# A pre-norm block with hedgehog linear attention and a gated FFN: four re-orderings in the opening, the key/value loop and the FFN

## The chip, the cores and the metric

The kernel runs on one core of a Trainium2 chip. The metric is the device time of one execution in microseconds (us). The times before are three runs of the same kernel; one further execution was taken by the hardware profiler and left the profile that is read here. Engines are named as the profile names them: PE is TensorE (PEld its weight loads), DVE is VectorE, ACT is ScalarE, POOL is GpSimd, SP is SyncE, which issues the DMAs.

## The reference

The input `x` has 2048 rows of 640 numbers, all tensors are bfloat16. There are 32 heads of 20 numbers, and the FFN is 1536 wide.

```python
ln = layernorm(x)                                   # over 640, no scale or shift
q, k, v = split_heads(ln @ wqkv)                    # 32 heads of 20
pq, pk = q @ w_phi[h], k @ w_phi[h]                 # per head, 20 x 20
phi_q = concat([softmax(pq), softmax(-pq)], -1)     # 40 numbers for each head
phi_k = concat([softmax(pk), softmax(-pk)], -1)
kv  = einsum("bhsf,bhsd->bhfd", phi_k, v)           # summed over all 2048 rows
z   = einsum("bhsf->bhf", phi_k)
num = einsum("bhqf,bhfd->bhqd", phi_q, kv)
den = einsum("bhqf,bhf->bhq", phi_q, z)[..., None] + 1e-6
h   = x + (num / den) @ wo
out = h + (gelu(layernorm(h) @ w_gate) * (layernorm(h) @ w_up)) @ w_down
```

The attention is not causal: every row's `phi_q` needs `kv` summed over all rows. So all 16 tiles must have passed the key/value stage before the first row's attention can be finished.

## The kernel before, in words

The 2048 rows are 16 tiles of 128 rows, four tiles to a block. A tile `t` passes these steps in the first half of the kernel:

- `ln_st` (lines L109 to L127) takes the statistics of one or two tiles. For a pair it is four `bn_stats` and two `bn_aggr` on DVE, then on POOL `ve` (variance plus eps, L121), `rstd` (L122) and one `mr` for each tile (L127).
- `ln_ap` applies the normalisation, in one instruction on ACT (L133) or DVE (L138). Its result is transposed into `LN1T`, either by a DMA that SP issues (L149) or, for the first tiles, by `ln_tp`, five matmuls on TensorE and a copy (L146, L147).
- `v_mm` and `v_ev` compute `v` (matmuls L272, eviction on ACT L292 to one of eight `vS` buffers).
- `k_tile` computes `pk` with the folded weight `Wk2` (the product of `w_phi` and the key weight, made by `fold`, L227 to L238) and takes the two exponentials, of `pk` and of `-pk`, on ACT (L305), to `E`.
- `k_norm` turns them into normalised values: `sk`, a reduce over 20 numbers on DVE (L312), `rs`, its reciprocal on DVE (L316), and `vt`, which is `v` times `rs`, once for each sign `s` (L320). The key's softmax denominator is so put on `v`. The half `s = 1` runs on POOL. The half `s = 0` runs on POOL too for the tiles in the tuple `VP`; for the others it runs on DVE, and it is not issued at once: it is kept in `todo` and issued in the next tile's `k_norm`, between `sk` and `rs`. The last tile's `s = 0` is issued on DVE at once.
- `kv_tile` adds a tile's part of `kv` and `z` in PSUM (`kvp`, L338). These matmuls stand in groups, after tiles 5, 9, 13 and 15 and behind the loop for tiles 12 to 15. `kv_mask` then forms the block matrix `KV` (L346 to L350).

Each engine runs its instructions strictly in the order in which the code issues them: nothing is re-ordered by a scheduler (`manual_schedule`). A wait on one engine so holds up all that is queued behind it. PSUM tiles of the projections are taken in rotation (`gtile`): four buffers up to tile 2, three in the rest of the loop, and four again in the attention; a matmul that starts a new tile waits until the buffer's last reader is done.

The opening treats tiles 0 to 5 by hand. The loop `for t in range(NT)` then does for each tile: `k_tile(t)`, in some tiles a `fold` for the query weight or query projections (`q_mm`, `q_exp`), `kv_tile` of earlier tiles, `v_mm(t + 4)`, `ln_ap(t + 6)` on ACT, `v_ev(t + 4)`, in even tiles the statistics of tiles `t + 8` and `t + 9`, and `k_norm(t)`.

Behind the loop come the query projections that are left, interleaved with the first tiles' attention, then the FFN. `attn_a` (L532, L552) multiplies a tile's `phi_q` with `KV` into `ab`, two PSUM tiles, and copies them to `AB`; `attn_b` to `attn_b3` divide; `attn_c` (L604) multiplies by `wo`; `attn_d` to `attn_e` add the residual, normalise and transpose to `LN2T`. `gate_up` (L664 to L670) and `down` (L683 to L689) are the FFN. `weave` deals the attention steps of later tiles out among the FFN's units: a step with offset `n` is issued ahead of unit `n`, and a unit is one `gate_up` or one half `down`.

Of the kernel before, what the change touches and what calls it, by code (L numbers as in the profile page):

```python
# [10 lines left out]
ALU = mybir.AluOpType  # L11
# [6 lines left out]
def kernel(  # L18
# [12 lines left out]
    nc = tc.nc  # L31
    P = 128
    S = 2048
    D = 640
    H = 32
    Dh = 20
    FF = 1536
    NT = S // P
# [5 lines left out]

    H0 = [(P * c) // Dh for c in range(NC)]
    NH = [(P * c + P - 1) // Dh - H0[c] + 1 for c in range(NC)]
    VP = (0, 2, 4, 6, 9, 11)
    KA, QA = (0, 2, 4), (0, 1, 2, 3, 4)
    LQ = (7, 8, 9, 9, 10)
    FQ = (10, 11, 12, 13, 14)  # L50
# [6 lines left out]
    VC = Dh + 1  # L57
# [3 lines left out]
    UH = H // 2  # L61
# [37 lines left out]
    def gtile(name):  # L99
        return psG.tile([P, 2, 512], F32, name=name, tag="G")  # L100
# [58 lines left out]
    Wk2 = p1.tile([P, NC, D], BF16, name="Wk2")  # L159
    acc = p1.tile([P, NC, 4, VC], F32, name="acc")  # L160

    vS = [p1.tile([P, H, VC], BF16, name=f"vS{i}") for i in range(8)]
    fp_cm = tc.tile_pool(name="fp", bufs=1, side="right", reuse_waits="tile")
    fp = fp_cm.__enter__()
    WkT = fp.tile([P, NC, D], BF16, name="WkT")
# [47 lines left out]
    def fold(WT, W2, halves, ds=range(NC)):  # L213


        runs = []
        for c in range(NC):
            lo, hi = H0[c] * Dh, (H0[c] + NH[c]) * Dh
            for u in range(2):
                a, b = max(lo, u * HD), min(hi, (u + 1) * HD)  # L220
                if a < b:
                    runs.append((u, c, a, b))
        runs.sort()
        for d in ds:
            wa = gtile("wa")
            for i, (u, c, a, b) in enumerate(runs):
                nc.tensor.matmul(wa[:, u, a - u * HD:b - u * HD], lhsT=WT[:, c, d * P:(d + 1) * P],  # L227
                                 rhs=BD[:, c].rearrange("p a b -> p (a b)")[:, a - H0[c] * Dh:b - H0[c] * Dh],
                                 start=(i == 0 or runs[i - 1][0] != u),
                                 stop=(i + 1 == len(runs) or runs[i + 1][0] != u), skip_group_check=True)  # L230
            dst, src = W2[:, d, :].rearrange("p (u f) -> p u f", u=2), wa[:, :, 0:HD]
            if halves:
                dst = W2[:, d, :].rearrange("p (c u f) -> p u c f", c=NC, u=2)
                src = src.rearrange("p u (c f) -> p u c f", c=NC)
            if d in (QA if halves else KA):
                nc.scalar.copy(dst, src)
            else:
                nc.vector.tensor_copy(dst, src)  # L238
# [13 lines left out]
    def ln_st(*tiles, act=True, between=None, log=False):  # L252
        for t, v in zip(tiles, ln_stats(p1, [x_sb[t // 4][:, t % 4, :] for t in tiles], "1", act, between, log)):
            lnp[t] = v

    def ln_ap(t, on_act=False, on_pe=False):
        ln = (ln_act if on_act else ln_dve)(p1, "1", *lnp[t])
        if on_pe:
            lnp[t] = ln
        else:  # L260
            transpose_to(LN1T[t // 4][:, :, t % 4 * P:(t % 4 + 1) * P], ln, False)

    def ln_tp(t, on_dve=False):
        transpose_to(LN1T[t // 4][:, :, t % 4 * P:(t % 4 + 1) * P], lnp[t], True, on_dve)
# [5 lines left out]
    def proj(ps, t, W, us=(0, 1), rows=False):  # L270
        for u, c in sorted(((u, c) for u in us for c in range(NC)), key=lambda x: x[::-1] if rows else x):
            nc.tensor.matmul(ps[:, u, 0:HD], lhsT=lnT(t, c), rhs=W[:, c, u * HD:(u + 1) * HD],  # L272
                             start=(c == 0), stop=(c == NC - 1))
# [3 lines left out]
    def v_mm(t, us=(0, 1)):  # L277
        if 0 in us:
            pv[t] = gtile("pv")
        proj(pv[t], t, Wv, us)  # L280
# [10 lines left out]
    def v_ev(t):  # L291
        nc.scalar.activation(vS[t % 8][:, :, 0:Dh].rearrange("p (u h) f -> p u h f", u=2),  # L292
                             pv[t][:, :, 0:HD].rearrange("p u (h f) -> p u h f", f=Dh), ACTF.Copy,
                             scale=lnp[t][2] if t in CT else 1.0)
# [5 lines left out]
    def k_tile(t):  # L300
        pk = gtile("pk")
        proj(pk, t, Wk2, rows=t == 0)
        Ek[t] = ev.tile([P, 2, D], BF16, name="E", bufs=8)
        for s in range(2):
            nc.scalar.activation(Ek[t][:, s, :].rearrange("p (u f) -> p u f", u=2), pk[:, :, 0:HD],  # L305
                                 ACTF.Exp, scale=((lnp[t][2], nrstd[t]) if t in CT else (1.0, -1.0))[s])

    def k_norm(t):


        sk = small(p1, [P, 2 * H], "sk")
        nc.vector.reduce_sum(sk, Ek[t].rearrange("p s (h f) -> p (s h) f", f=Dh), axis=AX.X)  # L312
        if t - 1 in todo:
            todo.pop(t - 1)()
        rs = small(p1, [P, 2 * H], "rs")
        nc.vector.reciprocal(rs, sk)  # L316
        Vt[t] = vt = ev.tile([P, 2, H, VC], BF16, name="vt", bufs=8)

        def mult(s, eng):
            eng.tensor_tensor(vt[:, s], vS[t % 8], rs[:, s * H:(s + 1) * H, None].to_broadcast([P, H, VC]), ALU.mult)  # L320

        mult(1, nc.gpsimd)
        if t in VP:
            mult(0, nc.gpsimd)
        elif t == NT - 1:
            mult(0, nc.vector)
        else:
            todo[t] = lambda: mult(0, nc.vector)

# [85 lines left out]
    v_ev(1)  # L415
    ln_st(4, act=False)
    ln_3()
    ln_ap(4, on_pe=True)
    v_part(2, *range(NC))
    v_ev(2)  # L420
    nc.sync.dma_start(x_sb[1][:, 2:4, :], x_v[:, 6:8, :])
# [1 line left out]
    nc.sync.dma_start(x_sb[3], x_v[:, 12:16, :])  # L423
    gtile('wu')
    ln_tp(3, True)
    fold(WkT, Wk2, False, (0, 1, 2))
    ln_tp(4, True)
    v_mm(3)
    ln_st(5, act=False)
    v_ev(3)  # L430
    fold(WkT, Wk2, False, (3,))
    v_mm(4)
    ln_ap(5, on_pe=True)
    fold(WkT, Wk2, False, (4,))
    v_ev(4)
    ln_tp(5)
    ln_st(6)
# [5 lines left out]
    for t in range(NT):  # L443
        if t == T3:
            ps_cm.close()
            psG = ps_cm.enter_context(tc.tile_pool(name="psG", bufs=3, space=PSUM, reuse_waits="tile"))
            psK = ps_cm.enter_context(tc.tile_pool(name="psK", bufs=1, space=PSUM, reuse_waits="tile"))
            kvp = psK.tile([P, 2, 512], F32, name="kvp")
        k_tile(t)
        if t == 0:  # L450
            ln_ap(6)
        if t in FQ:
            fold(WqT, Wq2, True, [i for i, f in enumerate(FQ) if f == t])
        for j in range(len(QT)):
            if t == QT[j]:
                q_mm(j)
                q_exp(j)
        for i in KVG.get(t, ()):
            kv_tile(i)
        if 0 < t < NT - 4:  # L460
            v_mm(t + 4)
        if t > 0 and t + 6 < NT:
            ln_ap(t + 6, on_act=True)
        if 0 < t < NT - 4:
            v_ev(t + 4)
        if t % 2 == 0 and t + 8 < NT:
            ln_st(t + 8, t + 9)
        k_norm(t)
        load_T(WqT, 0, *[i for i, f in enumerate(LQ) if f == t])
        if t == 10:  # L470

            for i in CT:
                ln_ap(i)
        if t == 9:
            nc.gpsimd.memset(KV, 0.0)
            nc.gpsimd.memset(kmask, 1.0)
            for r in HALF:
                nc.gpsimd.affine_select(out=kmask[r], in_=kmask[r], pattern=[[4, NC], [-Dh, 4]],
                                        compare_op=ALU.is_ge, fill=0.0, base=0, channel_multiplier=1)
                nc.gpsimd.affine_select(out=kmask[r], in_=kmask[r], pattern=[[-4, NC], [Dh, 4]],  # L480
                                        compare_op=ALU.is_ge, fill=0.0, base=Dh - 1, channel_multiplier=-1)
            nc.gpsimd.tensor_copy(KV[:, :, 0, :, KC - 1], kmask)
            nc.gpsimd.tensor_copy(KV[:, :, 1, :, 0], kmask)
        if t == 13:
            nc.sync.dma_start(Wg, wg_v)
            nc.sync.dma_start(Wo, wo_v)
            nc.sync.dma_start(Wu, wu_v)
# [60 lines left out]
    def attn_a(t, dve=0):  # L548
        attn_a_mm(t)
        AB, ab = ABs[t % 2], st[t, "ab"]  # L550
        for u in ((1, 0) if t in (5,) else (0, 1)):
            (nc.vector.tensor_copy if u >= 2 - dve else nc.scalar.copy)(  # L552
                AB[:, :, u * UH:(u + 1) * UH].rearrange("p s h f -> p s (h f)"), ab[u][:, :, 0:UH * KC])
        st[t] = AB
# [215 lines left out]
    def attn_at(t, i, offs):  # L770

        fns = (attn_a, attn_b, attn_b2, attn_b3, attn_c, attn_d, attn_d2, attn_e)
        return [(i + o, fn, t) for fn, o in zip(fns, offs) if o >= 0]

    SHORT = (0, 2, 3, 4, 9, 9, 10, 12)
    SHORT2 = (0, 2, 3, 4, 10, 10, 11, 13)
    LONG = (0, 1, 2, 5, 5, 6, 7)

    def attn_rest(t, i):
# [2 lines left out]


    weave(gus(0, 0, 256) + downs(0, (0, 1)),
          attn_at(2, 0, (-1, 0, 1, 2, 7, 7, 8, 10)) + attn_at(3, 1, (1, 2, 3, 4, 9, 9, 10, 12)) + attn_at(4, 6, SHORT2) + attn_at(5, 9, SHORT2) +
          attn_at(6, 13, SHORT2))
    weave(gus(0, 256, 512) + downs(0, (2, 3)),
          attn_at(7, 0, SHORT) + [(12, split), (14, attn_pair, 8), (16, attn_pair, 10)] + attn_rest(8, 15) +
# [37 lines left out]
```

## Time and profile before

| what | us |
|---|---|
| median of 3 runs (lowest, highest) | 277.12 (277.02, 277.51) |
| the profiled execution's own time | 278.27 |
| its span, first to last instruction | 276.4 |
| PE busy in the span | 271.0 (98%) |
| DVE busy | 176.8 (64%) |
| ACT busy | 139.2 (50%) |
| POOL busy | 97.2 (35%) |
| key/value loop, first `sk` to last `kvp` matmul | 21.7 to 71.1 |

The span is what the profile covers; the profiled execution took 1.9 us more than its span, and 1.15 us more than the median of the other runs. A row of the timeline has the start, the busy time of the instructions that were merged into it, the engine, the line, the operation, what it writes and reads, and their number (x3). What stands in brackets is the engine's idle time before it and what ended that. The granted TensorE clock is 1.00 throughout.

### The profile page before, as it was taken

What the parts mean: (1) busy time and instruction counts of PE and PEld (TensorE: products, weight loads), DVE (VectorE), ACT (ScalarE), POOL (GpSimd) and SP (SyncE); (2) the same over time, 40 slices, a digit from 0 to 9 for tenths busy, and PEclk for the clock granted to TensorE, in tenths of its full rate; (3) what the DMA queues carried; (4) which work ended last, traced back from release to release, by engine and by line L of the source; (5) the groups of instructions that cost most, each with busy time, mean ns of one, the idle gap of its engine ahead of it and who ended that gap; (6) DMA issues with size and microseconds to landing.
All of it is one profiled execution on the core that took longest, in us unless ns stands there. A gap on an engine that the chain in (4) does not pass through costs nothing.

```text
span 276.4 us, 5943 instructions
## 1 busy us (share of the span) xinstructions
PE 271.0 (98%) x2348; PEld 173.5 (63%) x2348; DVE 176.8 (64%) x335; ACT 139.2 (50%) x239; POOL 97.2 (35%) x218
## 2 busy tenths in 40 slices
PE   8999999999999999999999999999999999999995
PEld 4676767775455887788764555675555577444574
DVE  6889999999496776576477773346876333322322
ACT  4879897878489856365543255223245410223100
POOL 4238897774302316355303553102165400000000
PEclk9999999999999999999999999999999999999999
DMA  7963436489730021414111133110123111000011
GB/s 208 191 225 71 53 67 102 71 242 392 271 122 0 4 47 26 95 29 97 24 50 47 26 58 62 25 67 9 47 47 71 26 47 50 25 0 0 2 47 47
DMA packets 42235, 21.37 MB, mean 77 GB/s; under 512 B 35040, under 2 KB 40416, under 8 KB 42208
## 3 DMA queue, kind: packets, MB, share of 16 engines
q1 hardware_dynamic: 42208, 21.01, 30.1%
q8 instruction: 18, 0.29, 0.5%
q14 instruction: 9, 0.07, 0.1%
HBM read 10.18 MB, written 2.62 MB: 46 GB/s over the span
## 4 chain that ended last, share of the span: by engine, by line
PE 79%; DMA 5%; SPq 4%; issue 4%; DVE 3%; POOL 1%; ACT 1%; POOLq 0%; DVEq 0%
PE gu L664 38%; PE pd L683 19%; PE po L604 8%; PE pq L363 5%; PE pv L272 3%; PE ab L532 3%; SPq L186 3%; DMA LN1T<-ln 2%; DMA x_sb<-in_A_x_dram 2%; PE pk L272 2%; DMA WqT<-in_A_wqkv_dram 1%; DVE sk L312 1%; PE kvp L338 1%; DVE rs L316 1%; POOL vt L320 1%
## 5 line engine op out<-in xcount | busy, mean ns | idle before, releaser
L667 ACT ACTIVATE g<-gu 128x512 bf16<-128x512 f32 (+1 forms) x60 | 30.7, 512 | 68.6 <-PE gu L664 68.4
L670 DVE TENSOR_TENSOR GT<-gu,g 128x512 bf16<-128x512 f32 (+1 forms) x60 | 34.4, 580 | 47.9 <-PE gu L664 39.3
L664 PE MATMUL gu<-LN2T,Wg 128*128 128x512 bf16 (+1 forms) x300 | 61.8, 337 | 0.0
L664 PE MATMUL gu<-LN2T,Wu 128*128 128x512 bf16 (+1 forms) x300 | 61.8, 336 | 0.0
L683 PE MATMUL pd<-Wd,GT 128*128 128x320 bf16 (+2 forms) x396 | 53.5, 295 | 0.0
L683 PEld LDWEIGHTS <-GT 128*128 128x128 bf16 x396 | 37.9, 98 | 14.7 <-DVE GT L670 0.2
L664 PEld LDWEIGHTS <-Wu 128*128 128x128 bf16 x300 | 29.3, 98 | 22.6
L664 PEld LDWEIGHTS <-Wg 128*128 128x128 bf16 x300 | 28.8, 98 | 21.4
L272 PEld LDWEIGHTS <-LN1T 128*128 128x128 bf16 x290 | 27.7, 98 | 11.4 <-DMA LN1T<-ln 1.2
L686 DVE TENSOR_TENSOR y<-pd,x_sb 128x320 bf16<-128x320 f32 (+2 forms) x29 | 13.9, 480 | 29.0 <-PE pd L683 29.0
L320 POOL TENSOR_TENSOR vt<-vS,rs 128x672 bf16<-128x672 bf16 x22 | 29.1, 1344 | 9.1 <-DVE rs L316 7.4
L604 PE MATMUL po<-Wo,oT 128*128 128x320 bf16 x160 | 24.3, 299 | 0.0
L272 PE MATMUL pk<-Wk,LN1T 128*128 128x320 bf16 x160 | 24.2, 299 | 0.0
L363 PE MATMUL pq<-LN1T,Wq 128*128 128x512 bf16 x100 | 23.1, 379 | 0.0
L312 DVE TENSOR_REDUCE sk<-E 128x64 f32<-128x1280 bf16 x16 | 22.9, 1429 | 0.0
L368 ACT ACTIVATE Eq<-pq 128x1024 bf16<-128x1024 f32 (+1 forms) x26 | 20.0, 829 | 1.7 <-PE pq L363 1.7
L272 PE MATMUL pv<-Wv,LN1T 128*128 128x320 bf16 x130 | 19.8, 299 | 0.5 <-DMA LN1T<-ln 0.4
L604 PEld LDWEIGHTS <-oT 128*128 128x128 bf16 x160 | 15.6, 98 | 7.4 <-ACT oT L147 0.5
L305 ACT ACTIVATE E<-pk 128x640 bf16<-128x640 f32 x28 | 18.2, 705 | 3.9 <-PE pk L272 3.8
L581 DVE TENSOR_TENSOR tt<-AB,w 128x1280 bf16<-128x1280 f32 x12 | 17.9, 1488 | 1.1 <-POOL w L574 0.9
L133 ACT ACTIVATE ln<-x_sb,v,rstd 128x640 bf16<-128x640 bf16 x14 | 12.9, 920 | 10.7 <-POOL v L643 10.3
L363 PEld LDWEIGHTS <-Wq 128*128 128x128 bf16 x100 | 9.4, 98 | 10.0
(110 smaller groups left out, 292.9 us busy)
## 6 DMA issues: line engine op xcount, KB each, us to landing
out_dram<-y SPq DMA_DIRECT2D x15, 160.0 KB, 1.8
Wg<-in_B_w_gate_dram SPq DMA_DIRECT2D x1, 1920.0 KB, 7.7
Wu<-in_B_w_up_dram SPq DMA_DIRECT2D x1, 1920.0 KB, 13.6
Wd<-in_B_w_down_dram SPq DMA_DIRECT2D x1, 1920.0 KB, 7.8
x_sb<-in_A_x_dram SPq DMA_DIRECT2D x2, 640.0 KB, 7.0
Wo<-in_A_wo_dram SPq DMA_DIRECT2D x1, 800.0 KB, 9.3
x_sb<-in_A_x_dram SPq DMA_DIRECT2D x4, 160.0 KB, 3.2
Wv<-in_A_wqkv_dram SPq DMA_DIRECT2D x2, 320.0 KB, 4.2
```

Source lines behind the costliest of these rows:

```text
L272: nc.tensor.matmul(ps[:, u, 0:HD], lhsT=lnT(t, c), rhs=W[:, c, u * HD:(u + 1) * HD], start=(c == 0), stop=(c == NC - 1))
L305: nc.scalar.activation(Ek[t][:, s, :].rearrange("p (u f) -> p u f", u=2), pk[:, :, 0:HD], ACTF.Exp, scale=((lnp[t][2], nrstd[t]) if t in C ...
L312: nc.vector.reduce_sum(sk, Ek[t].rearrange("p s (h f) -> p (s h) f", f=Dh), axis=AX.X)
L320: eng.tensor_tensor(vt[:, s], vS[t % 8], rs[:, s * H:(s + 1) * H, None].to_broadcast([P, H, VC]), ALU.mult)
L363: nc.tensor.matmul(pqs[j][:, i, :], lhsT=Wq2[:, kc, c * P:(c + 1) * P], rhs=LN1T[b][:, kc, :], start=(kc == 0), stop=(kc == NC - 1))
L368: nc.scalar.activation(Eq[j][:, :, s, :], pqs[j][:, 0:len(QG[j])], ACTF.Exp, scale=(1.0, -1.0)[s])
L581: nc.vector.tensor_tensor(tt.rearrange("p s (h f) -> p s h f", f=Dh), num, w[:, :, :, None].to_broadcast([P, 2, H, Dh]), ALU.mult)
L604: nc.tensor.matmul(pos[u], lhsT=st[t][:, c, :], rhs=Wo[:, c, u * HD:(u + 1) * HD], start=(c == 0), stop=(c == NC - 1))
L664: nc.tensor.matmul(gu[i][:, 0:n], lhsT=W[:, c, f * P:(f + 1) * P], rhs=LN2T[b][:, c, a0:a1], start=(c == 0), stop=(c == NC - 1))
L667: nc.scalar.activation(g[:, 0:n], gu[0][:, 0:n], ACTF.Gelu_apprx_tanh)
L670: nc.vector.tensor_tensor(st[b, "g", f][:, a0:a1], gu[1][:, 0:n], g[:, 0:n], ALU.mult)
L683: nc.tensor.matmul(ps, lhsT=st[b, "g", f][:, tl * P:(tl + 1) * P], rhs=Wd[:, f, f0:f1], start=(f == 0), stop=(f == NF - 1))
```

## The change

Nothing is computed differently. The orders change in these places:

- Opening: tile 4's apply (on DVE) is issued behind tile 3's transpose and copy instead of ahead of them; tile 3's `v` comes ahead of tile 4's transpose; the statistics of tile 5 come ahead of tile 4's copy; two weight folds stand together.
- Loop: for `t` above 1, `ln_ap(t + 6)` is issued ahead of `k_tile(t)` and so ahead of the tile's exponentials on ACT. The statistics of tiles 10+11, 12+13 and 14+15 are issued in tiles 1, 3 and 5 instead of 2, 4 and 6.
- Tile 13's half `s = 0` of `vt` goes to POOL (`VP`). The last tile's half `s = 1` is shared: heads 0 to 15 on POOL, heads 16 to 31 on DVE behind its half `s = 0`.
- FFN: `attn_a` of tile 3 is issued ahead of unit 3 instead of unit 2, and its `attn_b`, `attn_b2`, `attn_b3` a unit later too. The order of the two PSUM copies is reversed for tile 4 instead of tile 5.

```diff
-    VP = (0, 2, 4, 6, 9, 11)
+    VP = (0, 2, 4, 6, 9, 11, 13)
...
-        def mult(s, eng):
-            eng.tensor_tensor(vt[:, s], vS[t % 8], rs[:, s * H:(s + 1) * H, None].to_broadcast([P, H, VC]), ALU.mult)
-
-        mult(1, nc.gpsimd)
+        def mult(s, eng, a=0, b=H):
+            eng.tensor_tensor(vt[:, s, a:b], vS[t % 8][:, a:b],
+                              rs[:, s * H + a:s * H + b, None].to_broadcast([P, b - a, VC]), ALU.mult)
+
+        mult(1, nc.gpsimd, 0, UH if t == NT - 1 else H)
         if t in VP:
             mult(0, nc.gpsimd)
         elif t == NT - 1:
             mult(0, nc.vector)
+            mult(1, nc.vector, UH)
         else:
             todo[t] = lambda: mult(0, nc.vector)
...
     ln_3()
-    ln_ap(4, on_pe=True)
     v_part(2, *range(NC))
...
     ln_tp(3, True)
+    ln_ap(4, on_pe=True)
     fold(WkT, Wk2, False, (0, 1, 2))
+    v_mm(3)
+    v_ev(3)
+    ln_st(5, act=False)
     ln_tp(4, True)
-    v_mm(3)
-    ln_st(5, act=False)
-    v_ev(3)
-    fold(WkT, Wk2, False, (3,))
+    fold(WkT, Wk2, False, (3, 4))
     v_mm(4)
     ln_ap(5, on_pe=True)
-    fold(WkT, Wk2, False, (4,))
     v_ev(4)
...
+        if t > 1 and t + 6 < NT:
+            ln_ap(t + 6, on_act=True)
         k_tile(t)
...
-        if t > 0 and t + 6 < NT:
-            ln_ap(t + 6, on_act=True)
+        if t == 1:
+            ln_ap(7, on_act=True)
         if 0 < t < NT - 4:
             v_ev(t + 4)
-        if t % 2 == 0 and t + 8 < NT:
-            ln_st(t + 8, t + 9)
+        if t == 0 or t % 2 and t + 9 < NT:
+            ln_st(t + 9 - (t == 0), t + 10 - (t == 0))
         k_norm(t)
...
-        for u in ((1, 0) if t in (5,) else (0, 1)):
+        for u in ((1, 0) if t in (4,) else (0, 1)):
...
-          attn_at(2, 0, (-1, 0, 1, 2, 7, 7, 8, 10)) + attn_at(3, 1, (1, 2, 3, 4, 9, 9, 10, 12)) + ...
+          attn_at(2, 0, (-1, 0, 1, 2, 7, 7, 8, 10)) + attn_at(3, 1, (2, 3, 4, 5, 9, 9, 10, 12)) + ...
```

## The prediction

> **What bounds the kernel now.** I read the page first, then the busy time by stage, then the chain that ended last, then the rows of VectorE (DVE) and GpSimd (POOL) in the key/value loop.
>
> ```profile
> PE 271.0 (98%) x2348; PEld 173.5 (63%) x2348; DVE 176.8 (64%) x335; ACT 139.2 (50%) x239; POOL 97.2 (35%) x218
> ```
>
> TensorE looks like the only limit: 98% busy. The stages say otherwise (columns: window, then busy time of each engine):
>
> ```profile
> 20.00:45.00 25.00, 24.50 (x280) 17.50 (x279) 24.62 (x44) 22.79 (x35) 22.12 (x30) 1.00 0.41 65
> 45.00:70.00 25.00, 25.00 (x344) 17.18 (x343) 24.19 (x25) 20.13 (x30) 16.64 (x20) 1.00 0.76 226
> ```
>
> In the loop, 20 to 70 us, DVE is as full as TensorE. The chain shows which of the two decides the stage's end (start, us, what):
>
> ```profile
> 65.34 0.54 DVE rs L316
> 65.88 0.06 DVE sk L312
> ...
> 67.14 0.14 DVE vt L320
> 67.28 0.72 issue
> 68.00 0.55 DVE rs L316
> ...
> 68.71 1.98 POOL vt L320
> 70.68 0.04 issue
> 70.72 0.38 PE kvp L338 x10
> ```
>
> Row after row it runs on DVE (sk, rs, vt), ends with the last vt on POOL, and only then TensorE goes on, after 0.55 us of waiting. So until 70.7 us the DVE sequence sets the end, and every delay in it moves everything behind. TensorE's own list of waits holds four: 0.8 us at the start, this one, and 0.4 each at 6.01 and 22.61. None comes after 70.7, so a delay there is kept to the end.
>
> The DVE rows, and the POOL rows beside them:
>
> ```profile
> 23.16 0.55 DVE L316 RECIPROCAL rs<-sk 128x64 f32<-128x64 f32 x1
> ...
> 27.32 1.43 DVE L312 TENSOR_REDUCE sk<-E 128x64 f32<-128x1280 bf16 x1
> 28.67 0.85 DVE L320 TENSOR_TENSOR vt<-vS,rs 128x672 bf16<-128x672 bf16 x1
> 29.44 0.55 DVE L316 RECIPROCAL rs<-sk 128x64 f32<-128x64 f32 x1
> ...
> 45.94 1.40 DVE L320 TENSOR_TENSOR vt<-vS,rs 128x672 bf16<-128x672 bf16 x1
> ...
> 61.30 1.48 DVE L320 TENSOR_TENSOR vt<-vS,rs 128x672 bf16<-128x672 bf16 x1
> ```
>
> ```profile
> 23.86 3.86 POOL L320 TENSOR_TENSOR vt<-vS,rs 128x672 bf16<-128x672 bf16 x3 [0.38 <-DVE rs L316]
> 27.81 0.23 POOL L121 TENSOR_SCALAR ve<-mv 128x2 f32<-128x2 f32 x1
> 28.12 0.71 POOL L122 TENSOR_TENSOR rstd<-ve,nhalf 128x2 f32<-128x2 f32 x1
> 28.93 0.96 POOL L127 TENSOR_SCALAR mr<-mv,rstd 128x1 f32<-128x1 f32 x2
> ...
> 42.76 3.86 POOL L320 TENSOR_TENSOR vt<-vS,rs 128x672 bf16<-128x672 bf16 x3 [0.18 <-DVE rs L316]
> ```
>
> What to see: the same vt costs DVE 0.85 us where POOL runs no vt (28.67), and 1.40 or 1.48 where it does. At 45.94 POOL's three end at 42.76 + 3.86 = 46.62 and DVE's ends at 47.34; at 61.30 POOL's three (from 58.20) end at 62.06 and DVE's at 62.78. Each time DVE finishes 0.72 us after POOL: it stood still until POOL was done. The other way round, POOL's last vt (68.71, 1.97 us for 1.31) ends 1.17 after DVE's vt of 68.64 to 69.50. The reduce keeps 1.43 beside POOL's vt. So vt multiplications on the two engines exclude each other, and before the change POOL's vt of tiles 1, 3 and 5 were over when DVE reached its own.
>
> **Statistics a tile earlier (the main term).** The statistics of tiles 10+11, 12+13 and 14+15 move from tiles 2, 4, 6 to tiles 1, 3, 5. On DVE this only permutes: reciprocal of the even tile, four statistics and two aggregates (25.56 to 27.32: 1.76), sk, rs, sk, then vt of the odd tile, at 28.67 as before. On POOL ve, rstd and mr move from behind the odd tile's vt to ahead of it. For tile 1: two vt from 23.86 (two thirds of 3.86, to 26.43), gap 0.09 and ve 0.23, gap 0.08 and rstd 0.71, gap 0.10 and two mr 0.50 (the pair at 22.98; the 0.96 above contains a wait for DVE's vt): 28.14. Then the odd tile's vt, 1.31, to about 29.46. DVE wants its vt at 28.67, is shut out, and ends at 29.46 + 0.72 = 30.18 instead of 29.52: 0.66 lost. POOL starts its pairs 0.15, 0.23 and 0.08 after the reciprocal's end in the three cases (23.86, 30.21, 36.41), so the losses are about 0.66, 0.74 and 0.59: 2.0 us. Bounds: nothing, if DVE is first (POOL leads by 0.5; a gain is excluded, since 0.85 is the least that a vt takes on DVE); and 2.9, if mr to vt takes 0.3 each time, as at 30.21. I take 2.0, since POOL's gaps are mostly 0.1 or less. From tile 6 on the phases between the engines are the old ones, only 2.0 later, and DVE has no idle time in which to recover: its gaps are 0.10 at most up to 69.5.
>
> **Tile 13's first half to POOL, last tile shared.** In the old time frame: POOL does three vt from 63.38, to 67.24. DVE saves its vt at 64.51 (0.91), runs sk and rs of 14 and sk of 15 to 66.56, wants vt of 14 at 66.48, waits for POOL and ends at 67.96, against 68.07. Of 0.91 saved, 0.11 is left. The last reciprocal ends at 68.43; DVE's vt goes to 69.39; then half a vt on DVE (0.43) and half on POOL (0.66) exclude each other. Either order ends at 70.2 to 70.3, against 70.68. The two edits give 0.43 together; side by side they would give 0.94, which I keep as the other end.
>
> The Trainium skill (SBUF — State Buffer, "Who interferes with whom") speaks against this edit: it calls the port pair of VectorE and GpSimd an exclusive lock, taken by a VectorE instruction with two SBUF inputs for its whole length, and says that a reduce never contends. By that rule the gain is the 0.43, and the 0.94 is excluded.
>
> **Applies ahead of exponentials.** Same instructions on ScalarE (0.92 apply, 1.30 for two exponentials, 0.70 v eviction), other order. The apply of tile 8 must wait for its mr (23.25), so the exponentials of tile 2 go from 22.75 to about 24.1. Queued behind: v of tile 6. They end at 25.4; TensorE wants that PSUM buffer at 25.33 (0.1 lost there); DVE wants E at 27.4 (nothing lost). At tile 8 the apply waits for mr until 42 and the exponentials end at 44.0; TensorE takes their buffer at 44.4. In return tile 12's transpose, queued on SP right behind the apply, lands 1 us earlier, and TensorE's 0.29 us at 40.20 (39.91 by the 1.36 spacing) goes. None of it counts, since TensorE then waits longer at 70; without DVE as cover it would be 0.2 us gained.
>
> **Opening.** Tile 4's apply and transpose go behind tile 3's copy and v: the 0.28 us wait ahead of the transpose at 12.74 goes, and v of tile 4 waits 0.1 to 0.2 us for a copy that now stands behind two statistics. The remaining 0.1 us disappears in the wait at 22.61, where tile 6's transpose, a chain from the x load issued at 11.83, sets the time. Zero; 0.2 either way without that cover.
>
> **FFN.** Between ab of tile 3 and the next gate/up 0.61 us pass (93.19 to 93.80) against 0.50 at 98.26: the buffer of the first gate/up is freed by GT at 93.74. A unit later that wait is gone: 0.11 gained. The tile's o and its transpose come 1.1 us later, with 2.3 us to spare before po at 105.10: nothing lost. The copy order of tiles 4 and 5 swaps: the buffers are wanted 2.45 us later (1.09 + 1.36), the two copies take 1.39; zero, or 0.7 without that cover.
>
> **Sum.** 2.0 - 0.43 - 0.11 = 1.5 us later. On the profiled execution (278.27, span 276.4): 279.8. That execution lies 1.15 above the median of the runs, so the difference goes onto the median: 277.1 + 1.5 = 278.6 us.
>
> **Rivals.** (1) POOL loses its lead: DVE's vt of tiles 1, 3, 5 start first, POOL waits, and DVE loses nothing. It decides at 28.67 and the two like it, if POOL's way from the second vt to the third takes over 2.2 us where I have 1.7. For it: the lead is only 0.5. Against: it is the same in all three pairs, and no row delays POOL by that. The tail's 0.43 to 0.94 and the FFN's 0.11 then count: 276.0 to 276.6. Chance 0.12. (2) One or two of the three pairs collide, or less long: 0.1 to 0.8 later, 277.2 to 277.9. Chance 0.13. (3) A worse tail: TensorE now waits some 2 us in pieces, and its clock falls, or a late exponential stalls it as well. The first 4608 columns took 4.00 us where ten 512-column matmuls later take 2.16, so one more such spell costs about 2 us: 280 to 281. Against: the 0.55 us wait at 70.72 left the clock at 1.00. Chance 0.07. (4) The forecast, 278.0 to 279.3: 0.68. That the change does not happen as written I exclude: the built order shows the statistics, ve, rstd and mr moved on DVE and POOL as described.
>
> The Trainium skill (TensorE: Matmul & The Clock Gate, "What's actually happening") lets the clock fall only after an idle window of about 3.4 us. By that rule the third rival costs nothing, since matmuls of tiles 14 and 15 stand between the waits; no row here shows a wait that long.
>
> **Numbers.** A difference of 0.2% (0.55 us) is about what a measurement of this kernel can tell from none. Slower: forecast 0.68, third rival 0.07, and of the second 0.08: 0.83. Same: 0.05 of the second. Faster: 0.12. The range leaves out the first rival and most of the third: 277.0 to 279.8.
>
> **What would show it.** Right: DVE's vt of tiles 1, 3 and 5 at about 1.5 us instead of 0.85, each ending some 0.7 after a POOL vt; DVE's reciprocal of tile 6 about 2 us later than the 42.13 of before; the last ten kvp matmuls at about 72.3; the wait at 40.2 gone without gain. Wrong: these vt at 0.85, or DVE with idle time of over 0.5 us in the loop, or the last kvp before 70.7.

## The result, and the profile after

| | before | after |
|---|---|---|
| median of 6 runs each, us (lowest, highest) | 277.38 (277.02, 277.51) | 278.71 (277.96, 278.91) |
| profiled execution, us | 278.27 | 278.79 |
| its span, us | 276.4 | 277.1 |

The changed kernel is slower: 1.0042 times the time of before, 95% interval 1.0031 to 1.0054, which is 0.9 to 1.5 us. The forecast was 278.6 us and 1.5 us of difference. That 278.6 lies only 0.1 us from 278.71 is partly luck: the forecast stood on the 277.12 of three runs of before, six runs have 277.38, and the difference of the medians is 1.33, not 1.5.

The page, and the busy time by stage, hide it. TensorE is busy 97% of the span, and in the loop DVE is as full as it was; a wait inside an instruction counts as busy:

```profile
PE 270.1 (97%) x2335; PEld 173.2 (63%) x2348; DVE 179.0 (65%) x335; ACT 138.8 (50%) x239; POOL 95.6 (35%) x219
```

```profile
20.00:45.00 25.00, 25.00 (x284) 18.00 (x282) 24.72 (x41) 21.99 (x34) 19.06 (x28) 1.00 0.39 69
45.00:70.00 25.00, 24.34 (x328) 16.45 (x327) 24.48 (x26) 19.99 (x30) 17.99 (x22) 1.00 0.70 189
```

On the page DVE has 2.2 us more of work (179.0 against 176.8) with the same 335 instructions. The timeline shows where, most of it in three rows. First DVE, then POOL, tiles 0 to 6 of the loop:

```profile
22.60 0.55 DVE L316 RECIPROCAL rs<-sk 128x64 f32<-128x64 f32 x1
...
28.12 1.47 DVE L320 TENSOR_TENSOR vt<-vS,rs 128x672 bf16<-128x672 bf16 x1
...
35.09 1.45 DVE L320 TENSOR_TENSOR vt<-vS,rs 128x672 bf16<-128x672 bf16 x1
...
42.04 1.30 DVE L320 TENSOR_TENSOR vt<-vS,rs 128x672 bf16<-128x672 bf16 x1
43.27 0.54 DVE L316 RECIPROCAL rs<-sk 128x64 f32<-128x64 f32 x1
...
69.01 0.54 DVE L316 RECIPROCAL rs<-sk 128x64 f32<-128x64 f32 x1
69.65 1.83 DVE L320 TENSOR_TENSOR vt<-vS,rs 128x672 bf16<-128x672 bf16 x2
```

```profile
23.31 2.59 POOL L320 TENSOR_TENSOR vt<-vS,rs 128x672 bf16<-128x672 bf16 x2 [0.38 <-DVE rs L316]
25.99 0.23 POOL L121 TENSOR_SCALAR ve<-mv 128x2 f32<-128x2 f32 x1
26.30 0.71 POOL L122 TENSOR_TENSOR rstd<-ve,nhalf 128x2 f32<-128x2 f32 x1
27.11 0.50 POOL L127 TENSOR_SCALAR mr<-mv,rstd 128x1 f32<-128x1 f32 x2
27.57 1.31 POOL L320 TENSOR_TENSOR vt<-vS,rs 128x672 bf16<-128x672 bf16 x1
...
34.52 1.31 POOL L320 TENSOR_TENSOR vt<-vS,rs 128x672 bf16<-128x672 bf16 x1
...
41.32 1.31 POOL L320 TENSOR_TENSOR vt<-vS,rs 128x672 bf16<-128x672 bf16 x1
...
69.72 1.40 POOL L320 TENSOR_TENSOR vt<-vS,rs 128x336 bf16<-128x336 bf16 x1 [1.35 <-DVE rs L316]
```

POOL's single vt now starts 0.55, 0.57 and 0.72 us ahead of DVE's. DVE's three take 1.47, 1.45 and 1.30 us where 0.85 is the time of one alone, and each ends 0.71 us after POOL's (29.59 after 28.88, 36.54 after 35.83, 43.34 after 42.63). From the reciprocal of tile 0 to that of tile 6 it is 43.27 - 22.60 = 20.67 us, against 42.13 - 23.16 = 18.97 before: **1.70 us lost**. The row of before at the end of this stretch:

```profile
42.13 0.55 DVE L316 RECIPROCAL rs<-sk 128x64 f32<-128x64 f32 x1
```

The tail, as TensorE sees it:

```profile
67.84 2.10 PE L340 MATMUL kvp<-vt,E 128*64 128x84 bf16 x100
70.56 0.38 PE L340 MATMUL kvp<-vt,E 128*64 128x84 bf16 x10 [0.62 <-DVE vt L320]
71.17 0.20 PE L340 MATMUL kvp<-vt,E 128*64 128x84 bf16 x1 [0.22 <-POOL vt L320]
71.53 0.35 PE L340 MATMUL kvp<-vt,E 128*64 128x84 bf16 x9 [0.17 <-DVE vt L320]
```

In place of one wait of 0.55 for POOL there are three, which go DVE, POOL, DVE: the three pieces of the last tile come one after another. From the last reciprocal to the end of the waits it is 71.53 - 69.01 = 2.52 us, against 70.72 - 68.00 = 2.72.

### The profile page after: what moved, and what is told of

The parts are those of the page before. It is cut to its first block, busy times and chain, and to the rows that moved or that the text cites. A ratio compares the mean times of both kernels' runs of the same rounds, so it can differ in the third digit from the quotient of the medians.

```text
span 277.1 us, 5930 instructions
## 1 busy us (share of the span) xinstructions
PE 270.1 (97%) x2335; PEld 173.2 (63%) x2348; DVE 179.0 (65%) x335; ACT 138.8 (50%) x239; POOL 95.6 (35%) x219
## 4 chain that ended last, share of the span: by engine, by line
PE 88%; DVE 4%; issue 4%; DMA 2%; SPq 1%; DVEq 0%
PE gu L667 38%; PE pd L686 19%; PE po L607 8%; PE pv L272 6%; PE pk L272 6%; PE pq L365 5%; PE ab L535 3%; DVE sk L312 2%; DMA Wv<-in_A_wqkv_dram 2%; PE pv L288 1%; DVE rs L316 1%; PE kvp L340 1%; PE tp L146 1%; DVE vt L320 1%; PE wa L227 1%
## 5 line engine op out<-in xcount | busy, mean ns | idle before, releaser
L320 POOL TENSOR_TENSOR vt<-vS,rs 128x672 bf16<-128x672 bf16 (+1 forms) x23 | 29.9, 1318 | 11.0 <-DVE rs L316 8.3
```

What stands on the lines that cost most here:

```text
L320: eng.tensor_tensor(vt[:, s, a:b], vS[t % 8][:, a:b], rs[:, s * H + a:s * H + b, None].to_broadcast([P, b - a, VC]), ALU.mult)
```

## Where the two profiles start from

The spans differ by 0.7 us while the medians differ by 1.33. The reason is the first row of DVE's long sequence, the statistics of tile 6, which wait for the x load. The first row is the kernel before, the second a later execution of the same kernel, the third the changed one:

```profile
17.40 0.89 DVE L109 BATCH_NORM_STATS2 stats<-x_sb 128x6 f32<-128x320 bf16 x2 [1.11 <-DMA x_sb<-in_A_x_dram]
```

```profile
17.14 0.89 DVE L109 BATCH_NORM_STATS2 stats<-x_sb 128x6 f32<-128x320 bf16 x2 [1.00 <-DMA x_sb<-in_A_x_dram]
```

```profile
16.85 0.89 DVE L109 BATCH_NORM_STATS2 stats<-x_sb 128x6 f32<-128x320 bf16 x2 [1.02 <-DMA x_sb<-in_A_x_dram]
```

The load was issued at 11.82 or 11.83 in both kernels, and its reader started 0.55 us earlier in the profiled execution of after. Everything behind starts from there. So I compare spans after taking off that start: before 276.4 - 17.40 = 259.0 and 276.1 - 17.14 = 259.0; after 277.1 - 16.85 = 260.25. The difference is about 1.25 us (spans are given to 0.1), and that is what has to be explained.

The second profile of before was taken to test this:

> The kernel before, unchanged, profiled once more. If the two first profiles differ by 0.7 us in span where the medians differ by 1.33 because the first profile of before began late (its x load landed 5.55 us after its issue at 11.83, that of the changed kernel 5.00 us after), then this profile has the landing nearer to 16.8, the first reduce at about 21.1 instead of 21.69, and a span of about 275.7. The rival, that the changed kernel's opening brings the load forward by about 0.55 us, expects the landing at 17.4 and the span at 276.4 again.

Measured: 277.97 us, span 276.1, first statistic at 17.14. It fell between my two expectations: the load comes at various times, not only at two. The part that matters held. The sequence from there on is the same to 0.05 us, and reciprocal of tile 0 to tile 6 is again 18.97.

## Experiments

In these sessions the kernel before had a median of 277.58 us (23 and 35 runs).

**The statistics alone.** The kernel before, with one edit:

```diff
-        if t % 2 == 0 and t + 8 < NT:
-            ln_st(t + 8, t + 9)
+        if t == 0 or t % 2 and t + 9 < NT:
+            ln_st(t + 9 - (t == 0), t + 10 - (t == 0))
```

> The kernel before with one edit: statistics of tiles 10+11, 12+13 and 14+15 issued in tiles 1, 3 and 5. Exclusion theory: the DVE halves of vt of tiles 1, 3 and 5 take 1.3 to 1.5 us instead of 0.85, the last kvp matmuls come 1.6 to 1.9 us later, the time is 1.6 to 1.8 us above before (ratio 1.006). Rival, the loss comes from the applies ahead of the exponentials or from the opening: the time is that of before within 0.4 us.

Measured: 278.97 us, 1.0055 (1.0040 to 1.0069), that is 1.1 to 1.9 us slower; the 1.6 to 1.8 expected lie inside. DVE rows of this kernel, then POOL's:

```profile
22.10 0.55 DVE L316 RECIPROCAL rs<-sk 128x64 f32<-128x64 f32 x1
...
27.62 1.47 DVE L320 TENSOR_TENSOR vt<-vS,rs 128x672 bf16<-128x672 bf16 x1
...
42.77 0.54 DVE L316 RECIPROCAL rs<-sk 128x64 f32<-128x64 f32 x1
```

```profile
26.60 0.50 POOL L127 TENSOR_SCALAR mr<-mv,rstd 128x1 f32<-128x1 f32 x2
27.06 1.31 POOL L320 TENSOR_TENSOR vt<-vS,rs 128x672 bf16<-128x672 bf16 x1
```

The reciprocals lie 20.67 us apart, as in after, and DVE's vt ends at 29.09, 0.72 after POOL's. This one edit makes the whole loss; the rest of the change takes a part of it back. TensorE starts its last ten kvp matmuls 0.62 us later than before (70.72 there), in an execution whose statistics of tile 6 start 1.05 us earlier (16.35), so 1.67 us later in all, as expected:

```profile
71.34 0.39 PE L338 MATMUL kvp<-vt,E 128*64 128x84 bf16 x10 [0.79 <-POOL vt L320]
```

**Everything but the loop.** The changed kernel with the loop's statistics and applies where they were; opening, tail and FFN stay changed:

```diff
-        if t > 1 and t + 6 < NT:
-            ln_ap(t + 6, on_act=True)
         k_tile(t)
...
-        if t == 1:
-            ln_ap(7, on_act=True)
+        if t > 0 and t + 6 < NT:
+            ln_ap(t + 6, on_act=True)
...
-        if t == 0 or t % 2 and t + 9 < NT:
-            ln_st(t + 9 - (t == 0), t + 10 - (t == 0))
+        if t % 2 == 0 and t + 8 < NT:
+            ln_st(t + 8, t + 9)
```

> The changed kernel with the loop's two re-orderings undone (statistics in even tiles, applies behind the exponentials); opening, tile 13 and shared last tile, and FFN as changed. Exclusion theory: the three collisions are gone, the gains of the tail (0.3 to 0.4 us by the two profiles) and the FFN (0.1) are left: 0.4 to 0.6 us below before (ratio 0.998). Rival, the loss lies in the tail or the opening: still over 1 us above before.

Measured: 276.88 us, 0.9978 (0.9966 to 0.9991), 0.6 us faster than before and the lowest ratio of this study. DVE's vt of tile 1 is back at 0.85 us and the reciprocals at 18.97:

```profile
21.70 0.55 DVE L316 RECIPROCAL rs<-sk 128x64 f32<-128x64 f32 x1
...
27.22 0.85 DVE L320 TENSOR_TENSOR vt<-vS,rs 128x672 bf16<-128x672 bf16 x1
...
40.67 0.55 DVE L316 RECIPROCAL rs<-sk 128x64 f32<-128x64 f32 x1
```

How the 0.6 us divides among opening, tail and FFN this profile does not show: it began early (statistics of tile 6 at 15.94), and at the end TensorE was the bound, with its last 120 kvp matmuls run from 67.23 without a wait.

**Only POOL's order.** To separate "statistics early" from "POOL's small instructions early", the changed kernel with the statistics still in odd tiles on DVE, and `ve`, `rstd` and `mr` issued behind the odd tile's vt:

```diff
+        def on_pool():
+            if not log:
+                nc.gpsimd.tensor_scalar_add(ve, mv[:, :, 1], EPS)
+                nc.gpsimd.tensor_tensor(rstd, ve, nhalf[:, 0:n], op=ALU.pow)
...
+        on_pool() if defer is None else defer.append(on_pool)
...
-            ln_st(t + 9 - (t == 0), t + 10 - (t == 0))
+            ln_st(t + 9 - (t == 0), t + 10 - (t == 0), defer=None if t == 0 else held)
         k_norm(t)
+        while held:
+            held.pop(0)()
```

> The changed kernel with one edit: in tiles 1, 3 and 5 the small POOL instructions of the statistics (ve, rstd, mr) are issued behind the tile's vt, as before the change; the order on DVE and ScalarE stays that of the changed kernel. Exclusion theory: POOL's vt then starts at the odd tile's reciprocal and is over 0.0 to 0.1 us after DVE wants its own, the DVE vt take 0.85 to 0.95, and the time is 0.2 to 0.5 us below before. Rival, the moved statistics on DVE themselves cost the time: the time stays 1.3 us above before.

Measured: 278.43 us, 1.0028 (1.0015 to 1.0041): slower than before by 0.8, where I had expected a gain. The mechanism did what was expected. DVE's vt of tile 1, with POOL's now ahead of its small instructions (DVE row, then POOL rows):

```profile
28.71 0.91 DVE L323 TENSOR_TENSOR vt<-vS,rs 128x672 bf16<-128x672 bf16 x1
```

```profile
27.60 1.31 POOL L323 TENSOR_TENSOR vt<-vS,rs 128x672 bf16<-128x672 bf16 x1 [1.10 <-DVE rs L319]
29.00 0.71 POOL L124 TENSOR_SCALAR ve<-mv 128x2 f32<-128x2 f32 x1
```

POOL's `ve` takes 0.71 us here, 0.23 elsewhere: it starts while DVE's vt runs and ends 0.09 after it, so now POOL is the one that waits. All three of DVE's vt take 0.91, and the reciprocals are 42.36 - 23.19 = 19.17 apart, 1.50 less than in after. But a new wait took its place, which I had not seen. ScalarE's rows, and TensorE's list of waits:

```profile
30.91 0.92 ACT L136 ACTIVATE ln<-x_sb,mr,rstd 128x640 bf16<-128x640 bf16 x1 [2.30 <-POOL mr L128]
31.73 1.28 ACT L308 ACTIVATE E<-pk 128x640 bf16<-128x640 f32 x2
```

```profile
PE pv L275 <- ACT E L308: 1.9, 2, 1.1
```

The mr end 31.11 - 23.19 = 7.9 us after the reciprocal of tile 0 starts, where after has 27.61 - 22.60 = 5.0. The apply that waits for them stands ahead of the exponentials, these hold a PSUM buffer, and TensorE waits for it twice, 1.9 us in all. Later DVE too waits 0.94 us for E. In this kernel TensorE ran its last 120 kvp matmuls, from 69.84, without any wait: it had become the bound itself, so its lost time counted. The profiled execution is the slowest of twelve (279.22 us): its x load was issued 0.3 us later than in after (12.15), and TensorE waited 0.7 us for `Wv` in the opening. So its waits name the mechanism, and the next run tests what it costs.

**The same, with the applies behind the exponentials.** This tests that reading of the miss:

```diff
-        if t > 1 and t + 6 < NT:
-            ln_ap(t + 6, on_act=True)
         k_tile(t)
...
-        if t == 1:
-            ln_ap(7, on_act=True)
+        if t > 0 and t + 6 < NT:
+            ln_ap(t + 6, on_act=True)
```

> The changed kernel with the small POOL instructions of the statistics behind the odd tile's vt and with the applies behind the exponentials; the statistics still stand a tile earlier on DVE. Theory, the POOL order costs by exclusion and the applies' order costs by making exponentials wait for mr, and the statistics' place on DVE costs nothing: DVE vt of tiles 1, 3, 5 at 0.9, no TensorE wait for E in the loop, 0.4 to 0.7 us below before, as without the loop's re-ordering. Rival, the earlier statistics on DVE cost something by themselves: at or above before.

Measured: 277.24 us, 0.9987 (0.9973 to 1.0000), just under the lower edge of what I expected as a gain, and with an interval that touches 1. The wait for E is gone from TensorE's list, the vt stay at 0.91, the reciprocals are 41.48 - 22.32 = 19.16 apart:

```profile
27.84 0.91 DVE L323 TENSOR_TENSOR vt<-vS,rs 128x672 bf16<-128x672 bf16 x1
```

Two kernels that differ only in where the applies stand are so 1.0028 and 0.9987 of before, about 1.1 us apart. It stays behind the version without any loop edit by 0.0009, less than either interval is wide; between the reciprocals the three vt at 0.91 cost it 0.19 us. So the rival, that the earlier statistics cost something on DVE by themselves, is bounded but not excluded.

**The applies alone.** The kernel before with the applies ahead of the exponentials (the edit above, reversed) and the statistics left in even tiles:

> The kernel before with one edit: the applies of tiles 8 to 15 ahead of the tile's exponentials on ScalarE, the statistics in even tiles. Theory from the run with the other POOL order, where TensorE waited 1.1 and 0.8 us for exponentials that stood behind an apply, which stood waiting for mr: the same two waits, TensorE reaches the last tiles late, 0.5 to 1.5 us above before. Rival, the applies' order is hidden under DVE's sequence: the time of before within 0.3 us.

Measured: 277.49 us, 0.9998 (0.9986 to 1.0010). My theory missed and its rival held. The applies do wait for mr (ScalarE idle 0.82, 1.06 and 1.06 us ahead of them), but little of it reaches TensorE:

```profile
PE pv L272 <- ACT E L305: 0.3, 1, 0.3
```

It is one wait of 0.27 us, and TensorE just had it to spare while DVE set the time (reciprocals 18.97 apart). At the end hardly anything is left: this execution began early (statistics of tile 6 at 16.61), and TensorE lists no wait for the last vt.

```profile
67.78 2.52 PE L338 MATMUL kvp<-vt,E 128*64 128x84 bf16 x120
```

So the place of the applies costs nothing measurable by itself; it costs when mr come as late as in the kernel of "Only POOL's order".

**The tail alone.** The kernel before with `VP` including 13 and the shared last tile:

```diff
-    VP = (0, 2, 4, 6, 9, 11)
+    VP = (0, 2, 4, 6, 9, 11, 13)
...
-        mult(1, nc.gpsimd)
+        mult(1, nc.gpsimd, 0, UH if t == NT - 1 else H)
...
             mult(0, nc.vector)
+            mult(1, nc.vector, UH)
```

> The kernel before with the tail's edits alone: tile 13's first half of vt to POOL, the last tile's second half shared. Exclusion theory: DVE's vt of tile 14 now waits for POOL (1.45 instead of 0.93), so of the 0.91 saved about 0.1 is left; the last reciprocal 0.1 earlier, the last kvp matmuls 0.3 to 0.4 earlier, the time 0.3 to 0.4 us below before. Rival, the two engines work side by side: vt of tile 14 at 0.93 and 0.7 or more below before (TensorE's wait in the tail was 0.5).

Measured: 277.41 us, 0.9982 (0.9969 to 0.9994), 0.2 to 0.9 us faster. The vt of tile 14 pays for what tile 13 saves, and then the shared tile:

```profile
65.87 1.45 DVE L320 TENSOR_TENSOR vt<-vS,rs 128x672 bf16<-128x672 bf16 x1
67.25 0.54 DVE L316 RECIPROCAL rs<-sk 128x64 f32<-128x64 f32 x1
67.89 1.83 DVE L320 TENSOR_TENSOR vt<-vS,rs 128x672 bf16<-128x672 bf16 x2
```

The 1.45 is what decides against the rival; the interval alone, which reaches 0.9 us, would not. The last reciprocal comes 0.12 us earlier, counted from that of tile 6 (67.25 - 41.50 = 25.75, before 25.87). That the last kvp matmuls come 0.3 to 0.4 earlier this profile does not show: TensorE had waited 1.1 us for `Wv` in the opening and ran the last 120 from 68.03 without a wait, so it and not DVE was the bound.

**The opening alone.** The kernel before with the opening's new order (the opening's part of the diff, nothing else):

> The kernel before with the opening's order alone. Theory: the x load that tile 6 waits for is issued at the same time and lands when it will, so the time is that of before within 0.2 us. Rival, the opening brings the DVE sequence forward: 0.3 us or more below before, with the first statistics of tile 6 clearly before 16.9.

Measured: 277.93 us, 1.0002 (0.9988 to 1.0016). Nothing that can be measured: the interval is -0.3 to 0.4 us, wider than the 0.2 expected, and the medians differ by 0.35. In the profile 276.2 - 17.26 = 258.9 is the span less the start of tile 6's statistics, as before. Here the statistics waited 1.46 us for the x load. Where the load was there in time, the new opening shows: they start at 15.94 in the version without the loop's edits, and at 16.35, with the old opening, in the statistics alone. What that is worth in time was not tested.

The FFN's edits were not run alone: 0.11 us is less than an interval. They were read in the traces.

## Why the prediction was right, point by point

**The bound** was read rightly: DVE's sequence. The edits that lengthened it (after, statistics alone) cost time, and those that changed only TensorE's or ScalarE's waits (opening, applies) made no difference that the intervals show. How little TensorE is behind DVE the prediction did not say; the last section shows it.

**The main term** was right in mechanism and size in tile 1 (0.63 measured, 0.66 forecast: DVE ends 6.99 us after the reciprocal's start, before 6.36), and too large in tiles 3 and 5: 0.59 and 0.44 for 0.74 and 0.59. Together 1.66 us, and 1.70 between the reciprocals, for 2.0. The step that failed is the shift of 0.08 and -0.07 from tile 1 to the others. I let POOL's start vary between tiles but took DVE's way from tile 1; from reciprocal to vt it is 28.12 - 22.60 = 5.52 there, 35.09 - 29.52 = 5.57 and 42.04 - 36.47 = 5.57 in the others, and without a collision the vt ends 6.43 after the reciprocal instead of 6.36 (version without the loop's edits: 28.07 - 21.70 = 6.37, then 34.41 - 27.98 = 6.43; the profile of before has the same, 35.02 + 0.85 - 29.44 = 6.43, so it could have been read there). DVE arrives later, so it waits less. The rest is POOL, some 0.04 faster from pair to third vt than my sum of rows.

**Tile 13 and the shared tile** were forecast at 0.11 and 0.32. From the reciprocal of tile 6 to that of tile 15 it is 25.87 us before and 69.01 - 43.27 = 25.74 after: 0.13, right. The shared tile gave 2.72 - 2.52 = 0.20 (the last nine matmuls start at 71.53). There the sum was careless: after DVE's vt to 69.39, halves of 0.43 and 0.66 that exclude each other end at 70.48, not at 70.2 to 70.3; the run has them in between. The 0.94 of edits side by side never appeared. The Trainium skill (SBUF — State Buffer, "Who interferes with whom") says that whoever issues first keeps the shared ports for the whole instruction and the other blocks; the rows agree in both directions: POOL first in tiles 1, 3 and 5 (DVE's vt 1.30 to 1.47, each ending 0.71 after POOL's, which is not quite the 0.85 of a whole vt), DVE first in the last tile (POOL's half 1.40 us where half of 1.31 is 0.66). Its sentence that a reduce never contends agrees too: sk beside POOL's vt took 1.42 to 1.47.

**FFN:** between ab of tile 3 (95.07) and the next gate/up (95.57) there are 0.50 us, for 0.61 before: 0.11, as forecast.

**Opening and applies:** nothing measurable, as forecast, and the waits at 12.74 and 40.20 went without gain; TensorE's list in after has no wait for E. One thing was not foreseen: in after TensorE waits 0.6 us at 60.20 for a transpose of tile 0 or 1 that DVE's applies (at 53.50, before 52.37) delay. It was hidden, since DVE's vt came last at 71.5.

**The sum:** 1.70 - 0.13 - 0.20 - 0.11 = 1.26 us, and the spans less their starts differ by about 1.25. Forecast: 1.5; the runs have 0.9 to 1.5. The two mis-sized terms, 0.3 too much loss and 0.1 too much gain, partly cancelled. Put on the profiled execution instead of the median, the forecast would have been 279.8, a microsecond above the 278.79 of after's: that execution of before had a late x load. The marks named in absolute times (the last kvp at 72.3, the reciprocal of tile 6 about 2 us after 42.13) missed mostly for the same reason: they came at 71.53 and 43.27, after a start 0.55 us earlier; the rest is the two mis-sized terms.

**Rivals.** POOL never lost its lead (0.55 to 0.72), and three pairs collided, not one or two. The clock stayed at 1.00 in the loop with waits of 0.62 and, in the statistics alone, 0.79 us, so the third did not come. The granted clock alone is a weak sign: it reads 1.00 in the first 5 us too, where the first 4608 columns took 4.00 us. But the pq matmuls right behind the last kvp take 2.33 us in both kernels (from 71.04 before, from 71.82 after), so they ran at the same pace. The idle window of the Trainium skill (TensorE: Matmul & The Clock Gate, "What's actually happening") was not tested: no wait in the loop comes near it.

## What to carry to other kernels

Where two engines exclude each other on an operation, the order of small instructions on one of them decides whether the large ones meet: 1.4 us of short POOL work moved ahead of a vt, three times, cost 1.7 us on an engine whose own instruction count did not change. Measure such a loss between two fixed instructions of the bounding engine, not on the span, and read busy times with care: the lost time shows as work. And when an instruction's producer is moved later, look at what is queued behind the waiting consumer: the same re-ordering on POOL ended 0.3 us below the kernel before (with an interval that touches zero) with the applies behind the exponentials, and 0.8 above it with them ahead.

## What the runs showed that I had not expected

The x load of tiles 6 and 7, issued between 11.82 and 11.84, is waited for until 17.40 and 17.14 (before, twice), 17.26 (opening alone), 16.85 (after) and 16.57 (POOL's order with the applies behind). It moves the whole run where DVE sets the time, up to 0.83 us between these, which is more than most of the edits here are worth. In the statistics alone and the version without the loop's edits, with the same time of issue, DVE lists no wait for it: it was there by 16.35 and 15.94. Runs of the kernel before lie between 276.81 and 278.65 us; that this load is what spreads them was not tested. It is not the only thing that varies: TensorE waits in the opening for `Wv` in four of the ten profiles (0.2 to 1.1 us), in the others not at all, and in three the x load was issued later, at 12.15 to 12.37.

TensorE is close behind DVE. In the version without the loop's edits (statistics of tile 6 at 15.94), in the tail alone (16.77) and in POOL's order with the applies behind (16.57) it ran all 120 last kvp matmuls without a wait: with DVE some tenths faster, or started earlier, it is the bound, and further gains on DVE end there.
